# Two attention and MLP passes on one core: a buffer of its own for the rest of the keys, softmax sums half a step later, differences of x for two groups in the first pass

## The chip, the core and the metric

The kernel runs on one core of a Trainium2 chip. The metric is the device time of one execution in microseconds (us). TensorE (PE) multiplies matrices; VectorE (DVE), ScalarE (ACT) and GpSimd (POOL) work on tiles element by element; SyncE (SP) issues the transfers (DMA), one after the other, and an instruction that waits holds back all that stand behind it on its engine. In matmul rows a clock of 1.00 is the full 2.4 GHz and 0.50 the lower level, 1.2 GHz.

## The reference

Attention with pooled keys and values over 8 batches, 8 heads, 576 positions of 64, then two MLPs on 4608 rows of 512:

```python
k_p = k.reshape(B, H, Sp, pool, D).mean(axis=3)          # 576 keys -> 72
v_p = v.reshape(B, H, Sp, pool, D).mean(axis=3)
scores = scale * np.matmul(q, k_p.transpose(0, 1, 3, 2))
attn = np.exp(scores - np.max(scores, axis=-1, keepdims=True))
attn = attn / (np.sum(attn, axis=-1, keepdims=True) + 1e-09)
x = rows_of(np.matmul(attn, v_p))                        # 4608 x 512
x = ((1 / (1 + np.exp(-(x @ w_gate)))) * (x @ w_val)) @ w_out
h = x @ w2_in                                            # 512 -> 2048
out = (h * np.cos(h)) @ w2_out
```

## The kernel before

The 4608 rows are nine chunks of 512 columns, c = 0 to 8. Matrices stand as two parts each, a rounded high and a rest, and a product takes three matmuls. The program is written in the order in which each engine is to run it (a manual schedule), so the Python code's order is each engine's queue.

**First pass (about 0 to 540 us).** half_steps(c) does gate and value products of the first MLP for chunk c over six column blocks f (FIRST_F). Each f is two half steps: gv_step issues twelve matmuls for the gate, then calls `between`, which runs the list beside[n] of the half step, then issues twelve for the value, then gate_times on DVE (L727), and after it the list of the next half step runs. The lists hold the attention of chunk c + 1, laid out by plan(c + 1): q_step (transposes of q), s_step (scores, maximum on DVE, exponentials on ACT, sums and division on DVE by `normal`) at half step f + 1 of a tile, a_step (transposes of the weights, split into aT and aR) at f + 4, x_step (the product with the values, into xT and x_raw). They also hold the loads and poolings of keys and values of later batches: keys of batch b are loaded at half steps 6 and 7 and pooled on POOL at 9 and 11, two passes ahead of their scores, and k_step transposes the pooled keys (pk, pkr) at half step 0 of the next loop. A batch's 72 pooled keys are 64 (two raw tiles, buffers "kvraw") and a rest of 8 (one raw tile, "kvrest", shared by keys and values). v_step, at half step 8 or later, reads the rest of the values from that raw tile (vRp, vr).

**Beside it.** `keep_g` stores gated tiles (od<-g) and lets POOL form differences tg of two of them (L751); tg has one buffer in this pass, and its store (od<-tg, L754) is written four ticks later. A tick is a half step. `far` steps prepare weights of later passes (raw_gv, ro, so); `near` steps form the differences of x (x_sums) of a group of two chunks: three loads and later a fourth of 128 x 1024, four subtractions or additions on DVE (L664), four stores. Before the change, near does group 0 and, 24 half steps later, group 1.

**Last chunk and second pass.** half_steps(8) has no attention; its lists (last_put) fetch x of group 0 (xg), fill weight tiles (gw, by `fill`) and prepare the last two gv pairs (exponents on ACT, bits on DVE, `sums_of` on POOL). Then g_block runs the remaining six columns by a scheme with seven products for eight, group after group (0 to 4); later_steps does x_sums of groups 2 to 4 and the pairs of w_out in it. The passes behind (w_out, w2_in with cosine, w2_out) aren't touched.

Of the kernel before, what the change touches and what calls it, by code (L numbers as in the profile page):

```python
# [9 lines left out]
F32 = mybir.dt.float32  # L10
# [12 lines left out]
def attention_two_mlps(  # L23
# [383 lines left out]
    def kv_load(src, b, nm, g):  # L407

        name = f"raw_{nm}{b}_{g}"
        if g < 2:  # L410
            raw = at.tile([P, 2, 512], F32, tag="kvraw", name=name, bufs=2)
            rows = src[b].rearrange("(i z) (y j) d -> z y i (j d)", z=2, j=POOL)
            for z in range(2):
                nc.sync.dma_start(raw[z * KM:(z + 1) * KM], rows[z, :KM, 2 * g:2 * g + 2])
        else:
            raw = at.tile([P, 1, 512], F32, tag="kvrest", name=name)
            last = src[b, :, KM * POOL:, :].rearrange("h (y j) d -> h y (j d)", j=POOL)
            for z in range(2 if nm == "v" else 1):
                nc.sync.dma_start(raw[z * KM:(z + 1) * KM, 0], last)
        kvraw[nm, b, g] = raw  # L420
# [110 lines left out]
    def s_step(t):  # L531
        c, n = t
        e = at.tile([P, H, KEYS], F32, tag="e", name=f"e{c}_{n}", bufs=2)
        mx = at.tile([P, 16], F32, tag="mx", name=f"mx{c}_{n}", bufs=2)
        found = scores(t, "t", e)
        for g, (p, _) in enumerate(found):
            nc.vector.reduce_max(out=mx[:, 4 * g:4 * g + 4], in_=p, axis=AX.X, negate=True)  # L537
        for g, (p, half) in enumerate(found):
            for h in range(4):
                m = 4 * g + h  # L540
                nc.scalar.activation(half[:, h], p[:, h], AF.Exp, bias=mx[:, m:m + 1])  # L541
        sm = at.tile([P, 16], F32, tag="sm", name=f"sm{c}_{n}", bufs=2)[:, :H]
        nc.vector.reduce_sum(out=sm, in_=e, axis=AX.X)
        normal(t, e, sm, nc.vector)
# [228 lines left out]
    def plan(c):  # L773

        steps = [[] for _ in range(NF)]
        early = [[] for _ in range(NF)]
        tiles = [(c, n) for n in range(TILES)]
        at_ = {1: (3, 4, 6, 7), B - 1: (0, 1, 2, 4)}.get(c, (0, 1, 3, 5))

        def put(f, fn, *args):  # L780
            steps[f].append(lambda: fn(*args))

        nt = -(-KM * c // P)
        def put_early(f, fn, *args):
            early[f if c > 1 else 0].append(lambda: fn(*args))

        for n, t in enumerate(tiles):
            if n < 2:
                put_early(NF - 3 + n, q_load, t)
            else:  # L790
                put(max(at_[n] - 3, 0), q_load, t)
        if c < B:
            for g in range(3):
                if c > 1:
                    put_early(6 + (g > 0), kv_load, k, c, "k", g)
                    put_early(9 + (g == 2), kv_pool, c, "k", g, nc.gpsimd)
                    put(0 if g < 2 else 1, kv_load, v, c, "v", g)
                    put(3, kv_pool, c, "v", g, nc.gpsimd)
                else:
                    put(2, kv_pool, c, "k", g, nc.gpsimd)  # L800
                    put(4, kv_pool, c, "v", g, nc.gpsimd)
        order_ = []
        for n, t in enumerate(tiles):
            f = at_[n]
            order_.append((f, 1 if c == 1 else 2, q_step, (t,)))
            order_.append((f + 1, 2, s_step, (t,)))
            order_.append((f + 4, 1.5, a_step, (t,)))

        if c < B:
            order_.append((4 if c == 1 else 0, 0, k_step, (c,)))  # L810
        f = at_[nt - 1] + 5
        for i in range(KB):
            order_.append((f, 3, x_step, (c, 0, i)))
        if c < B:
            order_.append((max(8, f), 4, v_step, (c, nc.vector)))
            f = NF - 2 if 1 < c < B - 1 else NF - 1
            for i in range(KB):
                order_.append((f, 5, x_step, (c, 1, i)))
        order_.append((NF - 1, 7, lambda: afterwards(2, lambda: x_save(c)), ()))
        for f, _, fn, args in sorted(order_, key=lambda s: (s[0], s[1])):  # L820
            put(f, fn, *args)
        return steps, early
# [589 lines left out]
    with tc.manual_schedule():  # L1412
# [78 lines left out]
        gw_tags.extend(f"w{NSLOT - 6 + h}" for h in range(2))  # L1491
        gw_tags.extend(f"w{n}" for n in range(NF))

        def chain(*steps):
            for s in steps:
                yield from s

        far = far_weights()

        def near_steps():  # L1500
            yield from x_sums(0)
            for _ in range(NF * 2):
                yield
            yield from x_sums(1)

        near = near_steps()
        plans = [plan(c) for c in range(1, NC)]
# [1 line left out]
        def half_steps(c):  # L1509
# [11 lines left out]
            for at_f, f in enumerate(FIRST_F):  # L1521
                tick()
                if c == 0 and at_f not in (3, 5):
                    split()

                def both(n):
                    for step in beside[n]:
                        step()
                    if 0 < c < NC - 1:
                        next(far, None)  # L1530
                        next(near, None)
                    elif last:
                        last_steps(n)

                def between():
                    both(2 * at_f)
                    tick()

                gv_step(c, f, 1 if c == 0 and at_f < FIRST else None, between=between)
                both(2 * at_f + 1)  # L1540
                if c == 0 and at_f == 0:
                    for g in range(3):
                        kv_load(k, 1, "k", g)
                    for g in range(3):
                        kv_load(v, 1, "v", g)

        for c in range(NC - 1):
            half_steps(c)
        for _ in chain(far, near):
            pass  # L1550
        at.release()
        xq = tc.alloc_tile_pool(name="xq", bufs=1, side="left", reuse_waits="tile")
# [44 lines left out]
        for n in range(2):  # L1597
            def exponents(n=n):
                for raw in gv_raw[4 + n]:
                    stage_exponent(raw)  # L1600
            last_put(5 + n, exponents)
            last_put(6 + n, lambda n=n: stage_bits(gv_raw[4 + n]))
            last_put(7 + n, lambda n=n: sums_of(gv_raw[4 + n], nc.gpsimd))
        for n in range(2):
            last_put(2 + n, lambda n=n: gv_fill(7 + n))
            last_put(4 + 2 * n, lambda n=n: g_next(1, n))
        for n in range(10):
            last_put(2 + n, lambda n=n: gv_fill(9 + n))
        half_steps(NC - 1)
        gv.release()  # L1610
        gx[0] = tc.alloc_tile_pool(name="xe", bufs=1, side="left", reuse_waits="tile")
        zp = tc.alloc_tile_pool(name="zp", bufs=1, side="right", reuse_waits="tile")
# [52 lines left out]
                put(g, m, at[2], lambda g=g, j=j: x_low(("g", g + 1), ORDER[j], nc.vector))  # L1665

        def later_steps():
            for g in range(2, len(GROUPS)):
                yield from x_sums(g)
            for n in range(HF):  # L1670
                exponents, bits, sums, plain, rest = pair_of(
                    "o", n, [STAGING[0], STAGING[1], STAGING[2], STAGING[0]]
# [4 lines left out]
                        fn()  # L1677

        steps = later_steps()
        for g in range(final):  # L1680
            for m in range(NB):
                for pos in (0, 2, 4, 6) if g else (1, 4):
                    put(g, m, pos, lambda: next(steps, None))

        def finish_steps():
# [243 lines left out]
```

## Time and profile before

| | |
|---|---|
| median of three runs | 1799.83 us (1798.72 to 1801.77) |
| the profiled execution | 1800.33 us, span from first to last instruction 1798.6 us |
| busy: PE, DVE, ACT, POOL | 1694.7, 1176.1, 954.9, 651.4 us |
| mean granted clock of PE | 0.973 |
| DMA | 411.03 MB, mean 229 GB/s |

The page gives busy times, the span in 40 slices and the costliest groups. Behind it stand views of the trace: who waited for whom, timelines of an engine, and windows (busy time of each engine in a stretch). An idle engine costs nothing where PE is busy, so all is read from PE's waits.

### The profile page before, as it was taken

What the parts mean: (1) busy time and instruction counts of PE and PEld (TensorE: products, weight loads), DVE (VectorE), ACT (ScalarE), POOL (GpSimd) and SP (SyncE); (2) the same over time, 40 slices, a digit from 0 to 9 for tenths busy, and PEclk for the clock granted to TensorE, in tenths of its full rate; (3) what the DMA queues carried; (4) which work ended last, traced back from release to release, by engine and by line L of the source; (5) the groups of instructions that cost most, each with busy time, mean ns of one, the idle gap of its engine ahead of it and who ended that gap; (6) DMA issues with size and microseconds to landing.
All of it is one profiled execution on the core that took longest, in us unless ns stands there. A gap on an engine that the chain in (4) does not pass through costs nothing.

```text
span 1798.6 us, 27384 instructions
## 1 busy us (share of the span) xinstructions
PE 1694.7 (94%) x9432; PEld 1417.1 (79%) x9432; DVE 1176.1 (65%) x1823; ACT 954.9 (53%) x1844; POOL 651.4 (36%) x721
## 2 busy tenths in 40 slices
PE   7898898788998999999999999999999999999999
PEld 6776676667788877887788878888888878888887
DVE  7855666555567655565877587677767785655665
ACT  6444443444444444455665477777777854444433
POOL 3445336534245455442000006576868810000000
PEclk7898999999999999999999999999999999999999
DMA  9376379646458877777989787586778987666663
GB/s 257 101 215 176 99 211 295 200 127 189 156 202 298 275 257 237 253 232 226 311 283 298 236 272 245 185 261 222 249 240 287 316 286 248 209 221 215 206 218 123
DMA packets 304747, 411.03 MB, mean 229 GB/s; under 512 B 57056, under 2 KB 234976, under 8 KB 304608
## 3 DMA queue, kind: packets, MB, share of 16 engines
q1 hardware_dynamic: 304608, 409.29, 71.0%
q8 instruction: 74, 1.21, 0.3%
q14 instruction: 65, 0.53, 0.1%
HBM read 235.93 MB, written 173.28 MB: 228 GB/s over the span
## 4 chain that ended last, share of the span: by engine, by line
PE 55%; DMA 4%; DVE 2%; issue 1%; ACT 1%; POOL 1%; SPq 0%; DVEq 0%; ACTq 0%; POOLq 0%
PE py_A L1397 7%; PE py_B L1397 4%; PE py_A L1402 3%; PE pha L1053 3%; PE pha L1057 3%; PE pha L1058 3%; PE po_A L924 2%; PE po_A L925 2%; PE po_A L923 2%; PE py_B L1402 2%; DMA up<-od 2%; PE po_B L924 2%; PE po_B L925 2%; PE po_B L923 2%; PE py_C L1397 2%; PE phb L1058 2%
## 5 line engine op out<-in xcount | busy, mean ns | idle before, releaser
L65 DVE TENSOR_TENSOR sp<-sp,sp 128x1024 fp32r<-128x1024 f32 x126 | 149.8, 1229 | 83.7 <-ACT sp L1310 83.7
L65 DVE TENSOR_TENSOR up<-up 128x1024 fp32r<-128x1024 f32 (+1 forms) x98 | 116.8, 1196 | 70.7 <-ACT up L900 70.3
L65 POOL TENSOR_TENSOR x<-x 128x256 fp32r<-128x256 f32 x84 | 60.1, 748 | 271.3 <-ACT x L1016 271.0
L900 ACT CAST up<-up 128x1024 fp32r<-128x1024 f32 (+1 forms) x98 | 99.7, 1019 | 88.7 <-DMA up<-od 76.2
L1397 PE MATMUL py_A<-wy,sp 128*128 128x512 f32 x432 | 135.7, 395 | 0.0
L751 POOL TENSOR_TENSOR tg<-g 128x256 f32<-128x256 f32 x54 | 51.9, 961 | 231.2 <-DMA od<-tg 161.6
L1310 ACT CAST sp<-sp 128x1024 fp32r<-128x1024 f32 x126 | 124.0, 1056 | 1.8 <-DMA sp<-sd 1.8
L1053 PE MATMUL pha<-x,hw 128*128 128x512 f32 (+1 forms) x320 | 118.5, 370 | 2.5 <-ACT ph L1113 0.9
L1105 POOL TENSOR_TENSOR s_S<-z_a,z_a 128x512 f32<-128x512 f32 (+1 forms) x78 | 94.3, 1230 | 67.3 <-DVE z_a L1088 67.3
L1057 PE MATMUL pha<-x,hw 128*128 128x512 f32 (+1 forms) x320 | 117.7, 368 | 0.0
L1058 PE MATMUL pha<-x,hw 128*128 128x512 f32 (+1 forms) x320 | 117.7, 368 | 0.0
L1084 ACT ACTIVATE z_a<-z_a 128x512 f32<-128x512 f32 (+1 forms) x160 | 94.5, 591 | 29.5 <-DVE z_a L1077 28.8
L541 ACT ACTIVATE e<-psc,mx 128x72 f32<-128x72 f32 x256 | 57.8, 337 | 84.1 <-DVE mx L537 84.1
L751 POOL TENSOR_TENSOR tg<-g,tg 128x256 f32<-128x256 f32 x108 | 96.6, 895 | 4.2
L704 PE MATMUL pg<-xT,wg 128*128 128x512 f32 (+1 forms) x228 | 93.1, 408 | 5.2 <-ACT e L562 2.9
L1105 POOL TENSOR_TENSOR s_S<-z_a,s_S 128x512 f32<-128x512 f32 (+1 forms) x78 | 94.9, 1217 | 3.9 <-DMA sd<-s_S 1.0
L1402 PEld LDWEIGHTS py_A<-wy,sp 128*128 128x128 f32 x432 | 81.2, 188 | 19.2
L704 PE MATMUL pv<-xT,wv 128*128 128x512 f32 (+1 forms) x228 | 95.8, 420 | 0.0
L1189 PE MATMUL pga<-xg,gw 128*128 128x512 f32 (+1 forms) x240 | 90.2, 376 | 4.4 <-DVE pg L1204 3.0
L924 PE MATMUL po_A<-up,so 128*128 128x512 f32 (+1 forms) x240 | 89.6, 373 | 4.4 <-DVE up L65 4.2
L706 PE MATMUL pg<-xT,wg 128*128 128x512 f32 (+1 forms) x228 | 89.4, 392 | 3.4 <-DVE wg L65 3.4
L751 POOL TENSOR_TENSOR tg<-g,g 128x256 f32<-128x256 f32 x54 | 49.7, 921 | 118.2 <-DVE g L727 117.6
(226 smaller groups left out, 5144.6 us busy)
## 6 DMA issues: line engine op xcount, KB each, us to landing
sp<-sd SPq DMA_DIRECT2D x126, 512.0 KB
up<-od SPq DMA_DIRECT2D x168, 256.0 KB
sd<-s_S SPq DMA_DIRECT2D x128, 256.0 KB
od<-tg SPq DMA_DIRECT2D x54, 512.0 KB
sd<-z_a SPq DMA_DIRECT2D x96, 256.0 KB
raw_o<-in_moe_w_out_dram SPq DMA_DIRECT2D x28, 512.0 KB
xg<-gd SPq DMA_DIRECT2D x28, 512.0 KB
x<-xd SPq DMA_DIRECT2D x28, 512.0 KB
```

The lines of the kernel that those rows point to most:

```text
L65: engine.tensor_tensor(out=lo, in0=x, in1=hi.bitcast(F32), op=ALU.subtract)
L704: nc.tensor.matmul(p, wh, x[:, 0, kb], start=kb == 0, stop=False)
L751: nc.gpsimd.tensor_tensor(out=t[:, k], in0=x, in1=y, op=ALU.subtract)
L900: nc.scalar.copy(hi, lo.bitcast(F32))
L924: nc.tensor.matmul(p, wh, x[:, 1], start=False, stop=False, skip_group_check=True)
L1053: nc.tensor.matmul(p, wh, x[:, 0, kb], start=k in (0, 3) and kb == 0, stop=False, skip_group_check=True,)
L1057: nc.tensor.matmul(p, wh, x[:, 1, kb], start=False, stop=False, skip_group_check=True)
L1058: nc.tensor.matmul(p, wl, x[:, 0, kb], start=False, stop=kb == 1, skip_group_check=True)
L1105: engine.tensor_tensor(out=z[name], in0=z[x], in1=z[y], op=op)
L1310: nc.scalar.copy(hi[:, r], lo[:, r].bitcast(F32))
L1397: nc.tensor.matmul(p, x[0][:, m, s], w, start=fresh and m == 0, stop=False, skip_group_check=True,)
L1402: nc.tensor.matmul(p[:, :HALF], x[1][:, m, s], w[:, :HALF], start=False, stop=m == PAIRS - 1, skip_group_check=True,)
```

## The change

Five things. The rest of the keys and the rest of the values get a buffer each. `normal` leaves s_step and becomes n_step, at f + 2, ahead of the a_step and q_step of that half step. near does groups 0 to 3 from half steps 0, 38, 62 and 77 (counted from chunk 1), and its tail runs in the last chunk. The last two gv pairs are prepared one half step earlier, their differences on DVE. later_steps keeps group 4 and the pairs of w_out, and starts in gate group 1.

```diff
-            raw = at.tile([P, 1, 512], F32, tag="kvrest", name=name)
+            raw = at.tile([P, 1, 512], F32, tag=f"{nm}rest", name=name)
...
+        exps[t] = e
+
+    exps = {}
+
+    def n_step(t):
+        c, n = t
+        e = exps.pop(t)
         sm = at.tile([P, 16], F32, tag="sm", name=f"sm{c}_{n}", bufs=2)[:, :H]
         nc.vector.reduce_sum(out=sm, in_=e, axis=AX.X)
         normal(t, e, sm, nc.vector)
...
             order_.append((f + 1, 2, s_step, (t,)))
+            order_.append((f + 2, 1.2, n_step, (t,)))
             order_.append((f + 4, 1.5, a_step, (t,)))
...
-            yield from x_sums(0)
-            for _ in range(NF * 2):
-                yield
-            yield from x_sums(1)
+            n = 0
+            for g, start in ((0, 0), (1, 38), (2, 62), (3, 77)):
+                while n < start:
+                    n += 1
+                    yield
+                for _ in x_sums(g):
+                    n += 1
+                    yield
...
                         last_steps(n)
+                        next(near, None)
...
-            last_put(5 + n, exponents)
-            last_put(6 + n, lambda n=n: stage_bits(gv_raw[4 + n]))
-            last_put(7 + n, lambda n=n: sums_of(gv_raw[4 + n], nc.gpsimd))
+            last_put(4 + n, exponents)
+            last_put(5 + n, lambda n=n: stage_bits(gv_raw[4 + n]))
+            last_put(6 + n, lambda n=n: sums_of(gv_raw[4 + n], nc.vector))
...
         half_steps(NC - 1)
+        for _ in near:
+            pass
...
-            for g in range(2, len(GROUPS)):
-                yield from x_sums(g)
+            yield from x_sums(len(GROUPS) - 1)
...
-        for g in range(final):
+        for g in range(1, final):
             for m in range(NB):
-                for pos in (0, 2, 4, 6) if g else (1, 4):
+                for pos in (0, 2, 4, 6):
```

How the instructions stand on the engines. First SP at the load of the rest of the keys of batch 3 (raw_k_2), with what each row waits for, before:

```order
L414 DMA raw_k_1_1705<-in_k_dram 64x2x512 [waits Pool_49]
L414 DMA raw_k_1_1705<-in_k_dram 64x2x512 [waits DMAHW2_49]
L419 DMA raw_k_2_1708<-in_k_dram 64x1x512 [waits DVE_49,DMAHW3_49,Activation_49,Pool_49]
L754 DMA od_78<-tg_0_1467 128x4x256 [waits DMAHW4_49,Pool_49]
L667 DMA gd_83<-xs_a_1617 256x1x256 [waits DMAHW5_49]
```

and after (lines of the changed kernel, which stand seven lower from L543 on):

```order
L414 DMA raw_k_1_1705<-in_k_dram 64x2x512 [waits Pool_49]
L414 DMA raw_k_1_1705<-in_k_dram 64x2x512 [waits DMAHW2_49]
L419 DMA raw_k_2_1708<-in_k_dram 64x1x512 [waits DMAHW3_49]
L761 DMA od_78<-tg_0_1467 128x4x256 [waits DMAHW4_49,Pool_49]
L674 DMA gd_83<-xs_a_1617 256x1x256 [waits DMAHW5_49,DVE_49]
```

The places are the same; the load waits only for an earlier transfer, no longer for DVE, ACT and POOL.

Second DVE in the loop of chunk 2, around tile 2 of chunk 3 (mx: maximum; sm and a: sum and division; g_1 with pv: gate_times; aT: the split in the a_step of an earlier tile), before:

```order
L537 TENSOR_REDUCE mx_2_2115<-psc_2_1_2117 128x4 [waits PE_49]
L543 TENSOR_REDUCE sm_2_2144<-e_2_2114 128x8 [waits Activation_49]
L572 TENSOR_SCALAR sm_2_2144<-sm_2_2144 128x8 [waits DVE_49]
L575 RECIPROCAL sm_2_2144<-sm_2_2144 128x8 [waits DVE_49]
L578 TENSOR_TENSOR a_2_2148<-e_2_2114,sm_2_2144 128x512 [waits DVE_49]
L583 TENSOR_TENSOR a_2_2148<-e_2_2114,sm_2_2144 128x4x2x32
L727 SCALAR_TENSOR_TENSOR g_1_2085<-g_1_2085,pv_1_0_2156 128x512 [waits DMAHW2_49,PE_49,Pool_49]
L65 TENSOR_TENSOR aT_2100<-pa_1_2170,aT_2100 128x4x128 [waits Activation_49]
```

and after:

```order
L537 TENSOR_REDUCE mx_2_2115<-psc_2_1_2117 128x4 [waits PE_49]
L734 SCALAR_TENSOR_TENSOR g_1_2085<-g_1_2085,pv_1_0_2149 128x512 [waits DMAHW2_49,PE_49,Pool_49]
L550 TENSOR_REDUCE sm_2_2163<-e_2_2114 128x8 [waits Activation_49]
L579 TENSOR_SCALAR sm_2_2163<-sm_2_2163 128x8 [waits DVE_49]
L582 RECIPROCAL sm_2_2163<-sm_2_2163 128x8 [waits DVE_49]
L585 TENSOR_TENSOR a_2_2167<-e_2_2114,sm_2_2163 128x512 [waits DVE_49]
L590 TENSOR_TENSOR a_2_2167<-e_2_2114,sm_2_2163 128x4x2x32
L65 TENSOR_TENSOR aT_2100<-pa_1_2170,aT_2100 128x4x128 [waits Activation_49]
```

gate_times has gone ahead of the sum and the four instructions behind it; so it is, with this or other work, in 23 of the 32 tiles that the loops prepare.

Third DVE in the last chunk, at the last of the two late gv pairs (raw_gv; L158 and L163 are its bits, L324 its differences, gw tiles filled from pairs), before:

```order
L158 TENSOR_SCALAR raw_gv_5348<-raw_gv_5348 128x512 x2
L163 SCALAR_TENSOR_TENSOR raw_gv_5348<-raw_gv_5348 128x512 [waits DVE_49] x2
L65 TENSOR_TENSOR gw_5547<-raw_gv_5345,gw_5547 128x2x256 [waits Activation_49]
L65 TENSOR_TENSOR gw_5575<-raw_gv_5345,gw_5575 128x2x256 [waits Activation_49]
L727 SCALAR_TENSOR_TENSOR g_2_5556<-g_2_5556,pv_2_0_5579 128x512 [waits DMAHW1_49,PE_49]
```

and after:

```order
L324 TENSOR_TENSOR raw_gv_5375<-raw_gv_5375 128x256 [waits DVE_49] x3
L324 TENSOR_TENSOR raw_gv_5375<-raw_gv_5375 128x256
L158 TENSOR_SCALAR raw_gv_5378<-raw_gv_5378 128x512 x2
L163 SCALAR_TENSOR_TENSOR raw_gv_5378<-raw_gv_5378 128x512 [waits DVE_49] x2
L65 TENSOR_TENSOR gw_5560<-raw_gv_1_4900,gw_5560 128x2x256 [waits Activation_49]
L734 SCALAR_TENSOR_TENSOR g_7_5533<-g_7_5533,pv_7_0_5564 128x512 [waits DMAHW1_49,PE_49,Pool_49]
L65 TENSOR_TENSOR xg_3_5467<-xg_3_5467 128x512 [waits DMAHW2_49]
L324 TENSOR_TENSOR raw_gv_5378<-raw_gv_5378 128x256 [waits DVE_49] x3
L324 TENSOR_TENSOR raw_gv_5378<-raw_gv_5378 128x256
```

The bits stand a half step earlier (beside g_7 instead of g_2), and DVE has the eight differences L324 that POOL had.

## Rows read from the trace of the kernel before

**Rows 1.** The page: busy time and count; PE busy in 40 slices.

```profile
PE 1694.7 (94%) x9432; PEld 1417.1 (79%) x9432; DVE 1176.1 (65%) x1823; ACT 954.9 (53%) x1844; POOL 651.4 (36%) x721
...
PE   7898898788998999999999999999999999999999
```

**Rows 2.** Waits of PE, 60 to 540: engine, line, releaser: us, times, longest us.

```profile
PE pk L446 <- POOL kS L401: 19.0, 9, 4.0
PE px L620 <- DVE aT L65: 11.8, 10, 2.6
PE pkr L447 <- POOL kR L401: 9.1, 5, 4.0
PE pq L510 <- ACT e L541: 4.3, 3, 2.1
```

**Rows 3.** Windows, six first f: us, busy of five engines, clock, DMA, GB/s.

```profile
105.90:115.60 9.70, 8.99 (x71) 6.05 (x69) 3.84 (x9) 3.65 (x7) 9.15 (x14) 1.00 0.91 255
159.30:176.30 17.00, 9.92 (x71) 7.15 (x69) 7.20 (x12) 3.77 (x8) 16.14 (x21) 0.80 0.65 198
...
395.80:411.50 15.70, 10.26 (x71) 7.37 (x70) 2.74 (x7) 1.18 (x2) 11.94 (x18) 0.78 0.81 217
sum 90.00, PE 61.22 PEld 44.14 DVE 35.02 ACT 14.17 POOL 75.14; mean PE 10.20 PEld 7.36 DVE 5.84 ACT 2.36 POOL 12.52
```

**Rows 4.** Waits of SP's queue, 110 to 470.

```profile
SPq L419 <- DVE vRp L65: 69.8, 5, 16.4
```

**Rows 5.** Timeline of SP: start, us, instruction.

```profile
151.73 0.62 SPq L419 DMA_DIRECT2D raw_k<-in_k_dram  x1
152.46 0.39 SPq L754 DMA_DIRECT2D od<-tg  x1
...
208.71 0.40 SPq L754 DMA_DIRECT2D od<-tg  x1
```

**Rows 6.** Timeline of POOL; in brackets the idle time before and its end.

```profile
156.26 0.73 POOL L751 TENSOR_TENSOR tg<-g 128x256 f32<-128x256 f32 x1 [12.93 <-DMA od<-tg]
...
163.11 2.51 POOL L401 TENSOR_TENSOR raw_k<-raw_k 128x512 f32<-128x512 f32 x2
...
169.97 0.31 POOL L401 TENSOR_TENSOR kR<-raw_k 64x64 f32<-64x64 f32 x1
...
212.78 0.74 POOL L751 TENSOR_TENSOR tg<-g 128x256 f32<-128x256 f32 x1 [22.93 <-DMA od<-tg]
```

**Rows 7.** Timeline of PE at the second boundary.

```profile
166.20 0.41 PE L446 MATMUL pk<-ident,kS 128*64 128x128 f32 x2 [3.98 <-POOL kS L401]
```

**Rows 8.** Timeline of DVE: gate_times ahead of that boundary.

```profile
145.56 0.68 DVE L727 SCALAR_TENSOR_TENSOR g<-g,pv 128x512 f32<-128x512 f32 x1
```

**Rows 9.** Waits of DVE, 60 to 470.

```profile
DVE sm L543 <- ACT e L541: 44.6, 29, 1.6
```

**Rows 10.** L324, L664 by line: ns min/median/max, first and last start.

```profile
L324 DVE TENSOR_TENSOR raw_i<-raw_i x32: 415/426/428, 855.8 to 967.0; 128x256 f32<-128x256 f32 x32
L664 DVE TENSOR_TENSOR xs_a<-xs_a,xs_a x20: 678/1220/1741, 124.3 to 610.3; 128x1024 f32<-128x1024 f32 x16, 128x512 f32<-128x512 f32 x4
```

**Rows 11.** Window of the last chunk's end.

```profile
519.00:549.00 30.00, 26.01 (x128) 22.50 (x127) 29.44 (x34) 18.00 (x32) 21.66 (x19) 0.94 0.55 191
```

**Rows 12.** Waits of PE, 540 to 720.

```profile
PE pgb L1189 <- ACT gz_a L1201: 4.0, 1, 4.0
PE pga L1189 <- DVE pg L1204: 3.0, 3, 2.5
```

**Rows 13.** Timelines of DVE and POOL in the last chunk.

```profile
530.62 1.28 DVE L163 SCALAR_TENSOR_TENSOR raw_gv<-raw_gv 128x512 int32<-128x512 int32 x2
...
535.68 2.48 DVE L163 SCALAR_TENSOR_TENSOR raw_gv<-raw_gv 128x512 int32<-128x512 int32 x2
...
532.13 4.34 POOL L324 TENSOR_TENSOR raw_gv<-raw_gv 128x256 f32<-128x256 f32 x4 [2.05 <-ACT gw L349]
```

**Rows 14.** By tile, aT on DVE (columns as in Rows 10).

```profile
L65 DVE TENSOR_TENSOR aT<-pa,aT x36: 676/684/693, 24.2 to 498.6; 128x512 fp32r<-128x512 f32 x36
```

More of the change, by code (lines that the diff above doesn't have):

```diff
@@ L1492, in attention_two_mlps @@
         gw_tags.extend(f"w{n}" for n in range(NF))
-        def chain(*steps):
-            for s in steps:
-                yield from s
         far = far_weights()
         def near_steps():
-            yield from x_sums(0)
-            for _ in range(NF * 2):
-                yield
-            yield from x_sums(1)
+            n = 0
[6 more added lines that the diff above has]
+                    yield
         near = near_steps()
@@ L1548, in attention_two_mlps @@
             half_steps(c)
-        for _ in chain(far, near):
+        for _ in far:
             pass
```

## The prediction

> **What bounds the kernel now.** I read the page first: TensorE (PE) is busy 1694.7 of 1798.6 us, so 104 us of PE's idle time is what a change of order can win, and the slices show where it lies: nines from slice 13 on, sevens and eights among the first 12 [rows 1]. So the first pass matters. Then the list of who PE waited for, from 60 to 540 us: the reader should see two kinds. The largest is the keys: pk and pkr wait 19.0 + 9.1 = 28.1 us for GpSimd (POOL), which pools them. The second is VectorE (DVE) and ScalarE (ACT) being behind: 11.8 us for aT, 4.3 for e, and small ones [rows 2]. Third, the windows of one f of the first pass each, the one in which the keys of the next batch are transposed. All six issue the same 71 matmuls. The first takes 9.70 us at full clock, the second 17.00 and the last 15.70 us at a granted clock of 0.80 and 0.78 (a mean of the levels 2.4 and 1.2 GHz), since PE stood still in them; the sum of the six is 90.00 [rows 3].
>
> Why are the keys late? SyncE (SP) stood 69.8 us, five times, at L419, the load of the rest of the keys, for DVE's vRp [rows 4]. Values and keys share the one buffer "kvrest", and v_step reads the old values from it late in the chunk. At 151.73 the load goes out at last, and right behind it the store od<-tg that had been ready [rows 5]. POOL's next tg needs that store landed (one buffer "t"): it sat 12.93 us and then did tg, the gv differences and only then the keys, 163.11 to 170.28, while PE had come to pk at 162.2 (166.20 minus 3.98) [rows 6, 7]. The next boundary repeats it: store issued at 208.71, POOL resumes at 212.78 after 22.93 us [rows 5, 6]. The chain is v_step, SP, store, POOL, PE; the keys' own data is not the cause.
>
> **The change part by part.** *Own place for the rest.* The load at L419 loses its wait for DVE; its old user, the key pooling a chunk earlier, is long done. What is late next? At the boundary at 162.2 the store would go out a mean hold of 69.8 / 5 = 14.0 us earlier [rows 4], at 138.5, and land 3.8 us later, as the store issued at 152.46 released POOL at 156.26 [rows 5, 6]. So tg then waits for its g, which DVE finished at 145.56 + 0.68 = 146.2 [rows 8]. From there POOL needs what it needed before, 170.28 - 156.26 = 14.0 us (tg, gv differences, keys), so it ends at 160.3, 1.9 us before PE comes to the first key (162.2) instead of 8 behind. I take the window with keys in time as the price of a boundary without a wait: 90.00 - 6 x 9.70 = 31.8 us over the other five, clock included [rows 3]. I keep back 2 us, since the first boundary has so little to spare and PE will come to it earlier: **-30**. Bounds: 0 (POOL still last everywhere) and -31.8. The extra buffer costs space alone. SP's queue behind it (q loads, od stores, value loads) only gets earlier.
>
> *Sums of exponentials a half step later.* DVE waited 44.6 us, 29 times, at the sum for ACT's exponentials, 1.54 us each [rows 9]. The five instructions stay (32 tiles, as before), but in 23 of the 32 tiles other work, nearly always gate_times, now stands between the maximum and the sum (for the other nine the half steps lie so that nothing comes between). It covers its own 0.68 us [rows 8]: 23 x 0.68 = 16 us less idling; fully covered it would be 23 x 1.54 = 35. Some copies of xT also go ahead of the five. DVE is not PE's bound, so PE gets that only where it was waiting for DVE or for an ACT that waited for DVE: 11.8 + 4.3 = 16.1 us [rows 2]. Nothing that PE waits for is moved behind more work; a_step still has two half steps. I take somewhat less than half of it: **-6**, with 0 and -16 as ends.
>
> *Last two gv pairs on DVE.* Eight subtractions leave POOL for DVE and start a half step earlier. The same operation on DVE, for i2, takes 426 ns: 8 x 0.426 = 3.4 us on a DVE that is busy 29.44 of the 30 us from 519 to 549 [rows 10, 11]. Against that, ACT sat behind POOL's result there, and PE waited 4.0 us for ACT's gz_a [rows 12]. And DVE's pair of L163 took 1.28 us with POOL idle, 2.48 us beside POOL's L324 and tg [rows 13]; POOL's 4.34 us stretch and its twin disappear, so DVE gets most of its 3.4 us back. The Trainium skill ("Perfetto Trace Analysis", Optimizing Scalar/DVE Operations) speaks against such an edit: the two engines share an SBUF read port, so that moving work between them might not help. By that the pairs would be worth nothing here and the forecast would stand 2 us higher; by [rows 13] the partner of the collision is gone, so I keep my value.
>
> *Differences of x for groups 2 and 3.* Eight L664 at 1220 ns leave the first two gate groups [rows 10], where PE waited 3.0 us for DVE's pg, 2.5 of it in one stop [rows 12]. For this and the pairs together: **-5**, ends -9 and +3. In the first pass they add 8 x 1.22 = 9.8 us to DVE in batches 6 and 7, with the loads and stores of x on SP ahead of od stores. DVE is busy 65% over the whole span [rows 1], so most of it falls into gaps; I charge a fifth: **+2**, ends 0 and +9.8. The pairs of w_out keep almost their old place, since group 0's twelve yields, now gone, held most of the sixteen of x.
>
> **Sum**: -30 - 6 - 5 + 2 = -39 us on the profiled execution's 1800.33 us (span 1798.6 and 1.7 around it): 1761. The median of the three runs is 1799.83, 0.5 below; that is inside the rounding.
>
> **Rivals.**
> (a) *Keys only half in time.* POOL's queue is in order, and so sums that wait for DVE's ro stand between the keys in some chunks; the tg ahead of them waits for g. For: the 1.9 us of room at the first boundary. Against: it asks for a lateness of 3 us at every boundary where the one worked out has 1.9 to spare. Half of 31.8 stays: 1761 + 15 = 1776.
> (b) *The collision moves.* The pooling of keys, 7.2 us (163.11 to 170.28 [rows 6]) five times, now runs beside busy DVE work, not while DVE idles at the boundary. At the rate of [rows 13] DVE would lose half of up to 36 us, 18; if PE saw it all: 1761 + 18 = 1779. Against: the split that PE waits for most, aT, reads PSUM, and its 36 lie between 676 and 693 ns [rows 14], whatever POOL did. The Trainium skill ("SBUF — State Buffer", Who interferes with whom) has the rule behind it: a DVE instruction with two SBUF inputs and a GpSimd one that reads SBUF block each other. By [rows 13], 2.48 against 1.28 us, the trace agrees.
> (c) *More than counted.* Without the standstills the waits for DVE and ACT in the first pass go (-16), the gate stretch gives its -9 and x costs nothing: 1800.3 - 31.8 - 16 - 9 = 1743.5.
> (d) *Slower.* tg's wait is not SP's hold but the store's own landing or the DMA engines; then nothing changes at the boundaries, and 9.8 + 3.4 = 13.2 us more DVE work in stretches where PE waits for DVE is all that is left: 1800 + 7 (half of it) = 1807. It decides if the boundaries give back less than the 13.2 us that the added work can cost. Against: POOL resumed 4 us behind the issue both times (156.26 after 152.46, 212.78 after 208.71), so the landing itself is short.
> (e) *It does nothing*: the load finds another late semaphore; 1799.
>
> **How the numbers follow.** Forecast 0.61, (a) 0.13, (b) 0.07, (c) 0.10, (d) 0.06, (e) 0.03. Predicted: 1761. Range 1743 to 1782: it takes in the forecast's own bounds, (a), (b) and most of (c), and leaves out (d), (e) and the tails, some 0.17. Within 0.2% (3.6 us, about what a measurement of this kernel can tell) is (e) and a sliver: 0.04; slower is (d) and a sliver: 0.07; faster 0.89.
>
> **What would show it.** Right: no wait of SP at L419 for DVE vRp; pk and pkr wait under 3 us for POOL; the five windows shrink to 10 to 11 us, with the clock full in them; DVE's wait at the sum under 32 us; gz_a's and pg's waits under 3 us together. Wrong: POOL still idles before tg at half step 8 and up; or PE's waits for aT and xT grow by what the keys gave; or new waits of SP for the x stores reach q or the od stores in batches 6 and 7.

## The result: 1772.4 us, 28 us faster and not 39

The changed kernel takes 1772.41 us in the median of four runs (1771.25 to 1774.06), against 1800.80 (1798.72 to 1805.57) for the kernel before beside it: a ratio of 0.9839 (after to before; 95% interval 0.9818 to 0.9861). 1761 was forecast, with 1743 to 1782 as the range. The time lies in the range and the direction was right, but 11 us of the gain are missing; the rest of this document is about where they went. The profiled execution has a span of 1770.7 us, 27.9 less than the one before.

PE's waits in the trace of the changed kernel, 60 to 540 us (columns as in [rows 2]):

```profile
PE px L627 <- DVE aT L65: 29.3, 10, 5.7
PE pga L1197 <- DVE pg L1212: 4.0, 1, 4.0
PE pq L510 <- ACT e L541: 3.7, 3, 1.5
```

pk and pkr, 28.1 us before [rows 2], no longer wait for POOL at all. In their place PE waits 29.3 us for aT, 11.8 before. SP's hold at L419 [rows 4] is gone too. POOL still waits for the store of tg, 123.0 us in all against 152.0 before, but no longer so that the keys come late. The windows of the first f after each boundary (columns as in [rows 3]), the first of them the one that had its keys in time before as well, and then the sum of the five others, 163.1 to 394.2:

```profile
105.80:115.50 9.70, 8.98 (x71) 6.03 (x70) 3.82 (x9) 3.65 (x7) 2.97 (x5) 1.00 1.08 369
219.40:227.30 7.90, 7.90 (x71) 6.19 (x69) 2.65 (x7) 1.18 (x2) 4.57 (x6) 1.00 1.09 304
...
sum 39.20, PE 39.20 PEld 30.80 DVE 19.05 ACT 8.15 POOL 26.62; mean PE 7.84 PEld 6.16 DVE 3.81 ACT 1.63 POOL 5.32
```

In the five windows PE is busy all the time, 39.20 of 39.20 us at full clock. Before they took 90.00 - 9.70 = 80.3 us [rows 3], so the boundaries gave **41.1 us**, more than the forecast's bound of 31.8. But look at the f just ahead of each boundary, the last of its loop. Below these are numbered by the chunk whose attention they prepare, 2 to 6: the last f in the loop of chunk 1 is that of chunk 2. First one of the five windows and their sum before (150.4 to 395.8):

```profile
267.80:275.20 7.40, 7.40 (x42) 6.46 (x41) 3.52 (x8) 4.89 (x12) 2.68 (x4) 1.00 0.83 253
...
sum 47.80, PE 41.93 PEld 34.68 DVE 26.63 ACT 25.41 POOL 13.96; mean PE 8.39 PEld 6.94 DVE 5.33 ACT 5.08 POOL 2.79
```

and the same f and the sum after (147.4 to 386.4):

```profile
259.90:273.40 13.50, 10.40 (x43) 8.87 (x42) 9.94 (x17) 5.38 (x13) 5.91 (x9) 0.75 0.51 138
...
sum 73.90, PE 52.34 PEld 44.66 DVE 48.68 ACT 26.95 POOL 41.19; mean PE 10.47 PEld 8.93 DVE 9.74 ACT 5.39 POOL 8.24
```

These five lost **26.1 us** with the same matmuls. PE's idle time in them rose from 47.80 - 41.93 = 5.9 to 73.90 - 52.34 = 21.6 us, by 15.7, and its busy time by 10.4, since the granted clock sits at the 1.2 GHz level for a while after each stop (0.75 in the row shown). DVE's busy time rose by 22 us (80 instructions lie in the windows instead of 62) and POOL's by 27.

What DVE did at one of them, in the stretch of v_step of batch 2 (vm, vRp, vr), before:

```profile
150.24 0.42 DVE L65 TENSOR_TENSOR vm<-vS,vm 64x256 fp32r<-64x256 f32 x1
150.68 0.92 DVE L65 TENSOR_TENSOR vRp<-raw_v,vRp 32x64 fp32r<-32x64 f32 x4
151.70 0.69 DVE L472 TENSOR_TENSOR vr<-vRp,mask 128x512 fp32r<-128x512 f32 x1
```

and after, DVE, then POOL in the same microseconds, then PE:

```profile
149.32 0.98 DVE L65 TENSOR_TENSOR vm<-vS,vm 64x256 fp32r<-64x256 f32 x1
150.32 3.58 DVE L65 TENSOR_TENSOR vRp<-raw_v,vRp 32x64 fp32r<-32x64 f32 x4
154.00 0.89 DVE L472 TENSOR_TENSOR vr<-vRp,mask 128x512 fp32r<-128x512 f32 x1
154.93 0.69 DVE L734 SCALAR_TENSOR_TENSOR g<-g,pv 128x512 f32<-128x512 f32 x1
155.53 0.68 DVE L65 TENSOR_TENSOR aT<-pa,aT 128x512 fp32r<-128x512 f32 x1
```

```profile
150.10 1.70 POOL L324 TENSOR_TENSOR raw_gv<-raw_gv 128x256 f32<-128x256 f32 x2
151.76 2.05 POOL L401 TENSOR_TENSOR raw_k<-raw_k 128x512 f32<-128x512 f32 x2
153.89 0.46 POOL L401 TENSOR_TENSOR kS<-raw_k 128x128 f32<-128x128 f32 x1
```

```profile
156.27 1.01 PE L627 MATMUL px<-aT,vm 128*128 128x384 f32 x2 [5.69 <-DVE aT L65]
```

Four splits of 32x64 that took 0.92 us together now take 3.58. Before, POOL stood still here, waiting for its store (idle until 156.26 [rows 6]); now the keys come in time because POOL does the gv differences and the keys in just these microseconds, and the splits of the values run beside it. aT itself takes 0.68 us as ever (by tile, ns min/median/max; before [rows 14]), but it stands behind them in DVE's queue, and PE waits 5.69 us for it:

```profile
L65 DVE TENSOR_TENSOR aT<-pa,aT x36: 676/683/692, 22.3 to 480.7; 128x512 fp32r<-128x512 f32 x36
```

The groups of DVE, 105 to 450 us (busy, mean ns of one), before and then after:

```profile
L65 DVE TENSOR_TENSOR vRp<-raw_v,vRp 32x64 fp32r<-32x64 f32 x20 | 4.4, 218 | 0.3
L65 DVE TENSOR_TENSOR vm<-vS,vm 64x256 fp32r<-64x256 f32 x10 | 4.2, 419 | 3.3 <-ACT vm L463 3.2
L472 DVE TENSOR_TENSOR vr<-vRp,mask 128x512 fp32r<-128x512 f32 x5 | 3.5, 692 | 0.6
```

```profile
L65 DVE TENSOR_TENSOR vRp<-raw_v,vRp 32x64 fp32r<-32x64 f32 x24 | 15.7, 655 | 0.3
L65 DVE TENSOR_TENSOR vm<-vS,vm 64x256 fp32r<-64x256 f32 x12 | 8.8, 733 | 2.8 <-ACT vm L463 2.7
L472 DVE TENSOR_TENSOR vr<-vRp,mask 128x512 fp32r<-128x512 f32 x6 | 4.9, 811 | 0.7
```

That is 24 x 0.437 + 12 x 0.314 + 6 x 0.119 = 15 us more for the same instructions, about the 15.7 us that PE stood longer.

The forecast's terms against the two traces:

| term | forecast | traces |
|---|---|---|
| first f behind a boundary, five | -30 (0 to -31.8) | -41.1 |
| last f ahead of a boundary, five | 0 (priced only as rival b) | +26.1 |
| the rest of chunks 1 to 7 (sums -6, x +2) | -4 | -2.8 |
| the gate groups up to w_out (pairs and x) | -5 | -9.8 |
| all other stages | 0 | -0.3 |
| sum | -39 | -27.9 |

(Chunks 1 to 7, from the first gate matmul of chunk 1 to that of chunk 8, went from 399.7 to 381.9 us; the gate groups' numbers are below.)

### The profile page after: what moved, and what is told of

It reads as the page before. It is cut to its first block, busy times and chain, and to the rows that moved or that the text cites. A ratio compares the mean times of both kernels' runs of the same rounds, so it can differ in the third digit from the quotient of the medians.

```text
span 1770.7 us, 27384 instructions
## 1 busy us (share of the span) xinstructions
PE 1688.7 (95%) x9432; PEld 1420.4 (80%) x9432; DVE 1188.8 (67%) x1831; ACT 954.7 (54%) x1844; POOL 633.6 (36%) x713
## 3 DMA queue, kind: packets, MB, share of 16 engines
q8 instruction: 74, 1.21, 0.3%
## 4 chain that ended last, share of the span: by engine, by line
PE 67%; DMA 4%; DVE 4%; issue 1%; ACT 1%; POOL 0%; SPq 0%; DVEq 0%; ACTq 0%; POOLq 0%
PE py_A L1405 7%; PE py_B L1405 4%; PE py_A L1410 4%; PE pha L1061 3%; PE pha L1065 3%; PE pha L1066 3%; PE pga L1197 3%; PE pga L1201 3%; PE pga L1202 3%; PE po_A L932 2%; PE po_A L933 2%; PE po_A L931 2%; PE py_B L1410 2%; PE po_B L932 2%; PE po_B L933 2%; PE po_B L931 2%
## 5 line engine op out<-in xcount | busy, mean ns | idle before, releaser
L758 POOL TENSOR_TENSOR tg<-g 128x256 f32<-128x256 f32 x54 | 46.4, 860 | 182.1 <-DMA od<-tg 123.0
L711 PE MATMUL pv<-xT,wv 128*128 128x512 f32 (+1 forms) x228 | 93.8, 411 | 0.0
L712 PE MATMUL pv<-xT,wv 128*128 128x512 f32 (+1 forms) x228 | 90.2, 396 | 0.0
```

The source lines that it names most:

```text
L711: nc.tensor.matmul(p, wh, x[:, 0, kb], start=kb == 0, stop=False)
L758: nc.gpsimd.tensor_tensor(out=t[:, k], in0=x, in1=y, op=ALU.subtract)
```

## The experiments

Two theories were set against each other. T1, collision: POOL's pooling, freed from its wait, runs beside v_step, and the stretched steps make aT late. T2: DVE is simply overloaded there, by the sums that were moved and by the added differences of x, or because PE now comes earlier.

### One part of the change at a time

Each kernel is the one before with one part.

**Own buffers for the rest alone.**

```diff
-            raw = at.tile([P, 1, 512], F32, tag="kvrest", name=name)
+            raw = at.tile([P, 1, 512], F32, tag=f"{nm}rest", name=name)
```

> The kernel before with one edit: own buffers for the rest of the keys and of the values. Two theories for why the whole change gave 28 us and not 39. T1 (collision): the keys come in time and the boundaries give about 41 us back, but POOL's key pooling now runs beside v_step on DVE, stretches its vm and vRp steps (0.42 and 0.22 us before) to a mean over 0.6 us and 0.5 us, and PE waits for aT in the last f of chunks 2 to 6, about 5 us each with the clock: 1800 - 41 + 25 = 1784, 1779 to 1789. T2 (DVE overloaded by the moved sums and the differences of x): this edit alone has neither, so it gives the whole of the boundaries, 1759 to 1768, vm and vRp keep 0.42 and 0.22 us, and PE's wait for aT stays near 12 us.

Measured: 1782.99 us, ratio 0.9898 (0.9866 to 0.9929): T1's number. This kernel has neither the moved sums nor the differences of x, and yet, from 60 to 520 us:

```profile
PE px L620 <- DVE aT L65: 26.4, 12, 5.5
```

```profile
L65 DVE TENSOR_TENSOR vm<-vS,vm x14: 416/856/1420, 93.5 to 433.5; 64x256 fp32r<-64x256 f32 x14
L65 DVE TENSOR_TENSOR vRp<-raw_v,vRp x28: 214/383/1241, 94.3 to 434.6; 32x64 fp32r<-32x64 f32 x28
```

The second fence is by tile (ns min/median/max): a split of 214 ns takes up to 1241. The last f of chunks 2 to 6 sum to 68.4 us here, 47.8 before, and the five first f behind the boundaries (166.0 to 393.4) to 39.5, 80.3 before:

```profile
sum 39.50, PE 39.50 PEld 31.05 DVE 23.77 ACT 9.20 POOL 26.16; mean PE 7.90 PEld 6.21 DVE 4.75 ACT 1.84 POOL 5.23
```

So the own buffers alone give 40.8 us back and charge 20.6 of the 26.1; the 20 us that are left are near the 18 of the ratio. T2, as far as it means the moved sums and x, falls as the main cause; that PE comes earlier is true here too, and the edits under "Taking the collision away" have to decide on it.

**Sums a half step later alone** (n_step and its line in plan).

> The kernel before with one edit: sums and division of a tile (n_step) a half step later. T1: nothing collides here; DVE's wait at the sum falls from 44.6 to about 17 us, PE gains a little, -1 to -6: 1794 to 1799. T2: the later sums put the division right ahead of a_step and v_step, PE's wait for aT rises by 5 us or more from 11.8: 1802 to 1808.

Measured: 1791.15 us, ratio 0.9946 (0.9928 to 0.9964), a gain beyond what either theory put there. DVE's wait at the sum falls to 21.1 us from 44.6 [rows 9]; PE's wait for aT falls too, from 11.8 to 8.2, so the moved sums delay nothing that PE needs. Where PE gains it is shown only in part: chunks 1 to 7 take 395.1 us instead of 399.7. The trace is 2.5 us ahead already when chunk 1 begins, but so is, by 2.0 us, that of the next kernel, which hasn't the moved sums.

**Differences of x alone** (near for groups 0 to 3, later_steps from gate group 1).

> The kernel before with one edit: differences of x of groups 2 and 3 in the first pass, later_steps from gate group 1 on. T1: the gate stretch loses the stop of 2.5 us for pg and its half clock (1.7 us), the first pass pays 0 to 2 us: 1796 to 1800. T2: 9.8 us more on DVE in chunks 6 and 7 are paid by PE by half or more, and SP's stores wait: 1800 to 1806.

Measured: 1801.31 us, ratio 1.0003 (0.9988 to 1.0018): no change, but from two large halves. The gate groups up to the first matmul of w_out before, in the changed kernel, and here:

```profile
538.20:813.90 275.70, 264.60 (x1256) 220.94 (x1256) 163.52 (x209) 124.55 (x212) 132.72 (x136) 0.99 0.77 256
```

```profile
520.40:786.30 265.90, 260.23 (x1255) 219.75 (x1254) 149.96 (x206) 123.12 (x210) 114.35 (x132) 0.99 0.71 235
```

```profile
551.30:816.70 265.40, 260.49 (x1255) 219.86 (x1254) 151.38 (x202) 124.54 (x213) 119.11 (x136) 0.99 0.71 234
```

The gate groups gain 10.3 us by this part alone, as much as in the whole change (9.8). Against that, chunks 1 to 7 cost 15.1 us more (414.8 against 399.7). One place of it, DVE ahead of aT and then PE:

```profile
321.67 1.22 DVE L664 TENSOR_TENSOR xs_a<-xs_a,xs_a 128x1024 f32<-128x1024 f32 x1
322.80 0.68 DVE L727 SCALAR_TENSOR_TENSOR g<-g,pv 128x512 f32<-128x512 f32 x1
323.40 0.68 DVE L65 TENSOR_TENSOR aT<-pa,aT 128x512 fp32r<-128x512 f32 x1
```

```profile
324.14 0.64 PE L620 MATMUL px<-aT,vm 128*128 128x320 f32 x1 [3.74 <-DVE aT L65]
```

A difference stands in front of the aT that PE waits for.

**The last two gv pairs alone.**

> The kernel before with one edit: the last two gv pairs a half step earlier, their differences on DVE. If POOL's turn was what held ACT's gz_a: the stop of 4.0 us and its half clock (1.7 us) go, 1793 to 1797. If it is DVE's load that counts there: the stop moves to pg or g and the time stays at 1799 to 1802.

Measured: 1798.61 us, ratio 0.9993 (0.9977 to 1.0009): no change that can be told. ACT's gz_a stops PE for 0.2 us instead of 4.6, and the wait moved to DVE, as the second half of the expectation says, though the time lies just under the range named there (PE, 520 to 720 us; before [rows 12]):

```profile
PE pga L1189 <- DVE pg L1204: 5.6, 3, 2.9
PE pgb L1193 <- DVE xg L65: 2.5, 2, 1.3
```

The four ratios make -1.02, -0.54, +0.03 and -0.07%, together -1.60%; the whole change has -1.61%. In the sum the parts add up, within an uncertainty of some 0.4% (an estimate from the four intervals).

**The whole change without the differences of x.**

> The changed kernel without the move of the differences of x (groups 2 to 4 in the gate pass, as before). Done alone, the move cost the first pass 15.1 us (from the first f of chunk 1 to that of the last chunk, 414.8 against 399.7) and gave the gate groups 10.2 back. If the same holds beside the other parts, the time is within 2 us of the changed kernel: 1770 to 1775, with the first pass some 7 to 15 us shorter and the gate groups some 10 longer. If the sums a half step later have made room for it on DVE, the move is a gain here: 1776 to 1782.

Measured: 1777.60 us, ratio 0.9884 (0.9861 to 0.9908), so beside the other parts the move of x is worth some 5 us by the medians; the intervals of the two ratios just overlap. So the agreement of the sum above is partly chance: three of the parts together give -1.16%, where their own ratios sum to -1.63. The two traces don't show the 5 us: their spans are 1770.9 us without the move, where the profiled execution lies 4.9 us under the median, and 1770.7 with it. In them chunks 1 to 7 take 376.9 us without it and 381.9 with it, and the gate groups 271.4 and 266.0, each by the same marks. The cost in the first pass is 5 us here, not 15; that the sums, moved, leave DVE the room is argued, not shown.

### Taking the collision away

Each of these is the changed kernel with one edit, or two where it says so. The table gives the windows of the last f of chunks 2 to 6 in each trace, which is where the collision was seen.

| kernel | chunk 2 | 3 | 4 | 5 | 6 | sum |
|---|---|---|---|---|---|---|
| before | 8.9 | 9.6 | 7.4 | 9.5 | 12.4 | 47.8 |
| changed | 15.7 | 14.8 | 13.5 | 14.5 | 15.4 | 73.9 |
| keys pooled at half step 7 | 18.8 | 10.0 | 7.5 | 8.0 | 11.5 | 55.8 |
| less pooling of keys | 15.5 | 10.0 | 7.5 | 13.9 | 14.5 | 61.4 |
| v_step at half step 7 | 10.3 | 13.8 | 13.0 | 14.9 | 16.6 | 68.6 |
| v_step on POOL | 9.0 | 8.0 | 9.2 | 13.6 | 13.7 | 53.5 |
| both of: keys at 7, v_step on POOL | 18.0 | 8.0 | 7.4 | 8.3 | 14.2 | 55.9 |
| POOL's instructions halved | 15.2 | 12.9 | 9.1 | 12.0 | 16.5 | 65.7 |

**Keys pooled earlier.**

```diff
-                    put_early(6 + (g > 0), kv_load, k, c, "k", g)
-                    put_early(9 + (g == 2), kv_pool, c, "k", g, nc.gpsimd)
+                    put_early(4 + (g > 0), kv_load, k, c, "k", g)
+                    put_early(7, kv_pool, c, "k", g, nc.gpsimd)
```

> The changed kernel, with the keys loaded two half steps earlier (4 and 5) and pooled on POOL at half step 7, ahead of the tg that waits for its store, so that the pooling lies before v_step and not beside it. T1 (collision with POOL's key pooling): vm and vRp on DVE return to 0.42 and 0.22 us (means below 0.5 and 0.3), PE's wait for aT falls from 29.3 to under 15 us, and the last f of chunks 2 to 6 lose 3 to 6 us each: 1750 to 1762. T2 (DVE is simply behind in that f, whatever POOL does, since PE comes earlier): vRp may shorten, but the time stays at 1768 to 1776 and the wait for aT above 22 us.

Measured: 1767.84 us, ratio 0.9821 (0.9805 to 0.9837), which overlaps that of the changed kernel. T1's numbers did not come: vm's mean is 0.64 us and vRp's 0.32 (105 to 450 us), PE's wait for aT is over the 22 us of T2, and the time 0.2 us under T2's range (60 to 510 us):

```profile
PE px L627 <- DVE aT L65: 23.8, 10, 8.7
```

By place, though, T1 holds. The windows of chunk 2, which has the longest of these waits, and of chunk 4:

```profile
147.40:166.20 18.80, 10.10 (x44) 8.77 (x43) 14.98 (x19) 5.17 (x11) 9.97 (x13) 0.82 0.61 153
...
263.10:270.60 7.50, 7.50 (x43) 6.51 (x42) 4.21 (x10) 4.89 (x12) 0.00 (x0) 1.00 0.63 166
```

In chunk 4 POOL does nothing in the window, v_step keeps its old durations (vRp 217 ns in chunks 3 and 4), and the f takes 7.50 us instead of 13.50. In chunk 2 the place of the keys on POOL is taken by tg and the gv differences, and the stop gets longer:

```profile
150.28 3.44 DVE L65 TENSOR_TENSOR vm<-vS,vm 64x256 fp32r<-64x256 f32 x2
153.74 3.38 DVE L65 TENSOR_TENSOR vRp<-raw_v,vRp 32x64 fp32r<-32x64 f32 x4
```

So it is not the keys but whatever POOL does. The five windows give back 18 us, but chunks 1 to 7 only 7.4 (374.5 us), and no gain of the whole is shown. The rest went between the windows: the four stretches from the start of one boundary's f to the next chunk's last f take 175.6 us here and 165.1 in the changed kernel, with DVE busy for 127.4 and 113.0 of them. Other steps of DVE with two operands in SBUF got longer in return; the division a<-e,sm 128x256 takes 530 ns in the mean before, 640 in the changed kernel and 735 here (60 to 530 us).

**Less pooling.** Two of three additions of each key pooling are left out.

> The changed kernel, with two of the three additions of each pooling of keys on POOL left out from batch 2 on (so the pooled keys are wrong, and POOL spends about 1.2 us instead of some 7 per batch at the same place in its queue). T1: the same as taking the collision away: vm and vRp near 0.42 and 0.22 us, 1748 to 1760. T2: 1768 to 1776.

Measured: 1762.78 us, ratio 0.9795 (0.9771 to 0.9819), 10 us under the changed kernel by the medians, where the intervals of the ratios just touch, and just above the expected range. Chunks 3 and 4 are back to where they were. Chunks 2 and 5 are not, since other work of POOL lies beside v_step there, the gv differences in 2 and tg in 5. Chunk 6 is not either, though POOL is busy for only 1.07 of its 14.50 us; but PE's wait for aT in it is as short as in the kernel before. First before, then here:

```profile
389.50 0.44 PE L620 MATMUL px<-aT,vm 128*128 128x128 f32 x2 [1.68 <-DVE aT L65]
```

```profile
369.97 0.69 PE L627 MATMUL px<-aT,vm 128*128 128x128 f32 x2 [1.68 <-DVE aT L65]
```

What chunk 6 has over the kernel before is a longer wait for ACT's part of aT (1.79 us against 1.12) and a lower clock (0.76 against 0.86). In the changed kernel that wait for DVE's aT is 3.21 us, 1.53 more, and vm and vRp take 3.29 us there instead of 1.76, also 1.53 more. In this chunk the stretched steps account for the whole of the longer wait, and T2 is not needed.

**v_step a half step earlier.**

> The changed kernel, with v_step from half step 7 on instead of 8 (it moves in four of the seven chunks). T1: there v_step runs ahead of the key pooling, and these chunks' last f lose about 3 us each; the other three stay: 1758 to 1768. T2: the same DVE work a half step earlier, DVE no less behind at the last f: 1770 to 1776.

Measured: 1774.53 us, ratio 0.9857 (0.9836 to 0.9878), the same as the changed kernel; T1's expectation fell. The rows of chunk 3, POOL and then DVE, tell why:

```profile
196.64 0.74 POOL L758 TENSOR_TENSOR tg<-g,g 128x256 f32<-128x256 f32 x1 [2.60 <-DVE g L734]
197.33 1.89 POOL L758 TENSOR_TENSOR tg<-g,tg 128x256 f32<-128x256 f32 x2
199.18 2.41 POOL L401 TENSOR_TENSOR raw_k<-raw_k 128x512 f32<-128x512 f32 x2
```

```profile
200.58 1.30 DVE L65 TENSOR_TENSOR vm<-vS,vm 64x256 fp32r<-64x256 f32 x2
201.89 2.98 DVE L65 TENSOR_TENSOR vRp<-raw_v,vRp 32x64 fp32r<-32x64 f32 x4
```

POOL's tg waits for gate_times, which stands on DVE some 4 us ahead of this: as POOL is released by DVE, its keys start where v_step starts. By the formula in the code the edit moves v_step in chunks 2, 3 and 4, one fewer than the expectation says; of these only chunk 2 escaped (10.3 us).

**v_step on POOL.**

```diff
-            order_.append((max(8, f), 4, v_step, (c, nc.vector)))
+            order_.append((max(8, f), 4, v_step, (c, nc.gpsimd)))
```

> The changed kernel, with v_step's seven splits and products on POOL instead of DVE (all chunks from 1 on). POOL then can't meet itself, and DVE loses 2.6 us of its own work per chunk. POOL needs 4.4 us for them, as it did for batch 0 in this trace (20.00 to 24.56). T1: the five last f of chunks 2 to 6 come back to within 1.5 us of the kernel before, the keys end 4.4 us later and still mostly in time: 1748 to 1760. T2 (DVE behind for other reasons): the wait for aT stays, 1766 to 1774. If POOL becomes the bound, pk or vr wait for it: 1772 to 1785.

Measured: 1767.50 us, ratio 0.9802 (0.9777 to 0.9826). Chunks 2 to 4 sum to 26.2 us, 25.9 before the change (chunk 4 alone is 1.8 us longer); PE's wait for aT is 9.5 us, the lowest but one of all these kernels. From chunk 4 on a new wait stands in its place, as the third case of the expectation has it, while the time lies in the range of T2 and its ratio still touches that of the changed kernel:

```profile
PE px L627 <- DVE aT L65: 9.5, 8, 2.5
PE px L627 <- POOL vr L472: 8.5, 4, 3.6
PE px L627 <- POOL vm L65: 3.0, 2, 1.9
```

**Both edits.**

> The changed kernel with both edits: keys pooled at half step 7 and v_step on POOL. T1: no wait of pk for POOL and none of aT in the last f of a chunk: 1745 to 1757, and at most as slow as either edit alone. If POOL's splits, now the last work before PE's px, come late, PE waits for vr or vm instead: 1760 to 1775.

Measured: 1765.91 us, ratio 0.9800 (0.9771 to 0.9829): no better than v_step on POOL alone. The second case: PE waits 7.5 us for vr and 3.8 for vm, and still 11.2 for aT.

**POOL's instructions halved.** `pooled` runs each addition for the two large key tiles in two halves.

> The changed kernel, with each of POOL's additions for the pooling of the two large key tiles (batch 2 on) cut into two of half the size: the same bytes, twice the instructions, at the same place. In the trace of the changed kernel a small DVE step beside them ends some 0.1 us after a POOL instruction ends, and so takes as long as one. If the two engines take turns by instruction, DVE's steps shrink with POOL's: vRp's mean from 0.655 to 0.35 to 0.5 us, and 1762 to 1769. If they share by bytes, vRp's mean stays at 0.6 to 0.7 us and the time at 1770 to 1775.

Measured: vRp's mean fell to 480 ns, in the range of turns by instruction (105 to 450 us, as above):

```profile
L65 DVE TENSOR_TENSOR vRp<-raw_v,vRp 32x64 fp32r<-32x64 f32 x24 | 11.5, 480 | 0.3
```

POOL's bytes are the same. vm's mean went from 733 to 676 ns and that of vr, of 0.69 us by itself, from 811 to 847, so only the small splits show it clearly. The time is 1769.45 us, but its ratio, 0.9839 (0.9819 to 0.9860), is that of the changed kernel: the five windows gain 8 us, and no gain of the whole is shown.

### A version that is faster

v_step on POOL where PE didn't wait for it, and the keys of batches 6 and 7 earlier:

```diff
-                    put_early(6 + (g > 0), kv_load, k, c, "k", g)
-                    put_early(9 + (g == 2), kv_pool, c, "k", g, nc.gpsimd)
+                    put_early((6 if c < 6 else 4) + (g > 0), kv_load, k, c, "k", g)
+                    put_early(9 + (g == 2) if c < 6 else 7, kv_pool, c, "k", g, nc.gpsimd)
...
-            order_.append((max(8, f), 4, v_step, (c, nc.vector)))
+            order_.append((max(8, f), 4, v_step, (c, nc.gpsimd if c < 5 else nc.vector)))
```

> The changed kernel, with v_step on POOL for batches 1 to 4 only (there PE never waited over 1.5 us for it, in batches 5 to 7 it waited up to 3.6 us for vr), and the keys of batches 6 and 7 loaded and pooled two half steps earlier (the two chunks where that took PE's stop in the last f away with v_step on DVE). By the windows of the single edits the last f of chunks 5 to 7 lose about 10 us less than with v_step on POOL everywhere: 1753 to 1764, faster than both kernels and than either edit alone. If POOL's work, moved once more, meets other DVE work: 1764 to 1770.

Measured: 1762.19 us, ratio 0.9795 (0.9775 to 0.9815), below the kernel before and the changed one (0.9818 to 0.9861). Against the single edits (0.9802, 0.9821) no difference is shown. The time lies in the expected range, but the last f of the five chunks sum to 51.3 us, only 2.2 less than with v_step on POOL everywhere, and chunk 6 is still at 14.2. PE waits 13.0 us for aT.

## Why the prediction was right in sign and 11 us off

- *The chain of the boundary* (v_step, SP, store, POOL, PE) was read rightly: without the shared buffer SP's hold, the lateness of the keys and PE's stop are all gone, and own buffers alone are the largest part (0.9898).
- *The price of a boundary* was 9.3 us too low in bound (41.1 against 31.8). The step that failed is the choice of the clean window: the f that had its keys in time takes 9.70 us in the changed kernel too, since its first gate matmuls wait for xT (they take 4.56 us, and 2.74 behind the boundary at 219.4); a boundary without a wait takes 7.8 to 7.9.
- *"The extra buffer costs space alone"* failed, and with it the 0.07 for rival (b). What happened is (b) in the main: POOL's work, the pooling above all, now runs beside DVE's v_step. (b) named the right rows [rows 13] and priced it at 18 us; the five windows lost 26.1, of them 20.6 with the own buffers alone. The forecast had put this term at nothing; that the whole is only 11 us off is partly luck, since the boundaries and the gate groups gave 16 us more than was forecast. The argument against (b) was that aT, reading PSUM, always takes 676 to 693 ns [rows 14]. That is still so after the change (676 to 692). But what counts is what stands ahead of aT on DVE: I looked at the instruction that PE waits for and not at its queue. The Trainium skill ("SBUF — State Buffer", Who interferes with whom) has just this distinction: a DVE instruction with two inputs in SBUF meets a GpSimd one that reads SBUF, an instruction of this kind (tensor_tensor) with a single input there does not, and the loser is blocked for the whole instruction. The trace agrees: vm, vRp and vr have two, and vRp goes from 214 ns up to 1248 in the changed kernel; aT has one.
- *The sums* were forecast at -6, with ends 0 and -16; alone they gave 0.54%, 9.7 us. The size was held too low. DVE's wait at them is 16.8 us in the changed kernel, under the 32 that were named; of PE's gain, the waits for aT show 3.6 us when it is done alone, and the rest is not traced.
- *The pairs and the differences of x*: -5 for the gate stretch, and it was -9.8. All but a part too small to measure is due to x, not to the pairs: alone the pairs give 0.9993. The Trainium skill's sentence ("Perfetto Trace Analysis", Optimizing Scalar/DVE Operations) that moving work between these two engines may not help agrees with this ratio; I had set it aside by [rows 13]. That the shared port is the reason here, no run shows. In the first pass x cost +2 by forecast, with +9.8 as the end, and 15.1 when it was done alone; in the whole change it cost some 5.
- *The signs to look for*: the hold, the keys and the wait at the sum came out as "right", and the windows fell even below the 10 to 11 us. gz_a and pg did not fall under 3 us together (4.0 us for pg in one stop remain, in the row of the first fence). And signs of "wrong" did appear: waits for aT grew by 17.5 us of the 28.1 that the keys gave; POOL still idled for the store ahead of a tg at half step 8 or later, for 11.9, 9.2 and 20.4 us in three chunks, though the keys were in time; and SP's waits for the stores of x (L667, later L674) rose from 10.7 to 81.9 us, of which no wait of PE for q is seen to have come.

Still open: what fills the 10.5 us that the stretches between the windows lose when the keys are pooled earlier, and the 5.5 us of the five windows that come only with the other parts of the change (without the differences of x they sum to 68.6). The longer divisions point to the same collision at other places; no run separates them.

## What to carry to other kernels

Before an engine is freed from a wait, list what it will then run beside: here POOL's standstill had kept its work away from DVE's two-operand steps, and the shared buffer, removed alone, gave 41 us at the boundaries and charged 21 ahead of them. When the time of an instruction that others wait for is constant, look at the queue ahead of it. And take the price of a clean stretch from several of its kind; one window can have a wait of another sort in it.

## What the hardware showed unexpectedly

A small DVE instruction beside POOL takes about as long as a whole POOL instruction, not a share longer: splits of 32x64 that take 0.214 us alone took 1.21 to 1.25 us beside POOL's instructions of 1.25 to 1.30, and 0.38 to 0.53 beside those of 0.45 to 0.53. And with POOL's instructions cut in half, at equal bytes, their mean fell from 0.655 to 0.480 us. Seven small steps were therefore a dear thing to put there. And the stops of PE for aT, of 3.1 to 5.7 us, were paid for again in clock, by two thirds: in the five windows 15.7 us of added idle time came with 10.4 us of added busy time for the same matmuls.
